# An emission order computed by a list scheduler, PSUM in single-bank tiles, and p loaded in 4 KB rows: attention feeding a swish MLP

## The chip, the cores and the metric

The kernel runs on one core of one Trainium2 chip. The metric is the device time of one execution in microseconds; I give the median of several runs with the lowest and highest. The kernel before took 307.49 us (306.49 to 308.46, 3 runs) when the prediction was made. In the profiles PE is TensorE, PEld its weight loads, DVE VectorE, ACT ScalarE, POOL GpSimd, and SP the engine that issues most transfers; a matmul's form such as 64*32 is the part of the array that it uses (rows*columns).

## The reference

Eight batches of eight heads, 576 positions of 64. A first attention packs keys and values into 32 rows per head with the queries p. A second one lets q attend to these rows, so its keys and its values are both the packed rows. The result, 4608 tokens of 512, goes through an MLP of width 2048 with `h * sigmoid(beta * h)`.

```
p_packed = sm_attn(p, k, v)               # 32 rows per head
out      = sm_attn(q, p_packed, p_packed)
x = out.transpose(0, 2, 1, 3).reshape(B * S, H * D)
h = x @ w_in                              # [4608,512] x [512,2048]
g = h * (1.0 / (1.0 + np.exp(-beta * h)))
return g @ w_out                          # [4608,2048] x [2048,512]
```

Both kernels use one idea: x is a product of the attention weights A2 and the packed rows, so the packed rows are multiplied by w_in first (W, small 64x32 tiles of the array), and h is A2 times W. beta is folded into W and divided out of w_out. In the profiles `w_ps` is that W product, `h_ps` the first and `o_ps` the second MLP product; `kT`, `qT`, `pT` are transposes; `s`, `z`, `pp` are scores, their sums and the packed rows.

## The kernel before

The order is written by hand: each phase interleaves one batch's MLP with the next batch's attention and the former batch's second product, by counts found by trial.

```python
self.ps_h = pool("ps_h", 2, space=PSUM)      # 2 tiles of 1 bank
self.ps_o = pool("ps_o", 2, space=PSUM)      # 2 tiles of 1 bank
self.ps_a = pool("ps_a", 2, space=PSUM)      # 2 tiles of 2 banks, all of the attention
...
def att(self, name, dtype=f32):
    n = 1024 if dtype == f32 else 2048       # two banks
...
def scores1(self, b):
    ps = self.att("s1_ps")
    for t in range(4):
        for c in range(NC): ...              # 16 matmuls into both banks
    nc.scalar.activation(E[:, 0:4, :], ps..., AF.Exp, scale=SCALE)   # then one activation
...
def fused_w(self, b, n):                     # W: eight 64*32 matmuls per group
    ps = self.att("w_ps").rearrange("p (r n) -> p r n", r=2)
    for c in range(NC):
        for r in range(2):
            self.mm(ps[32*c : 32*c+32, r, :], pp[64*r : 64*r+64, c, :],
                    self.w_in_bf[64*r : 64*r+64, c, cols], pos=(64*r, 32*c))
    ...                                      # one multiplication by beta on VectorE
...
nc.scalar.dma_start(self.p32[:], self.p.rearrange("b (g h) j d -> (h j) (b g) d", g=2))  # 256 B pieces
...
        attn("fused_w", nb, 0)               # the hand-made order, a few lines of one phase
        fill(6)                              # six steps of the former batch's second product
        main(10, 1)                          # one block of this batch's h, then one such step
        attn("weights2", nb)
```

The softmax here doesn't subtract the row's maximum and nothing guards it: scores larger than these inputs give would overflow.

Of the kernel before, what the change touches and what calls it, by code (L numbers as in the profile page):

```python
# [9 lines left out]
NP = 32  # L10
# [16 lines left out]
EXP_SET = "natural_log_exp_and_others"  # L27
SILU_SET = "silu_and_others"


class Kernel:
# [3 lines left out]
    def __init__(self, ctx, tc, q, k, v, p, w_in, w_out, beta, out):  # L35
# [16 lines left out]
        self.ps_a = pool("ps_a", 2, space=PSUM)  # L52
        self.x32, self.xbf = {}, {}
        self.st = {}
        self.g, self.grem = {}, {}
# [9 lines left out]
    def att(self, name, dtype=f32):  # L65
        n = 1024 if dtype == f32 else 2048
        return self.ps_a.tile([128, n], dtype, tag="att", name=name)


    def load(self, b, x, parts=1):  # L70
        nc, src = self.nc, self.src[x]
        t = self.in32.tile([128, 2304], f32, tag=f"{x}32", name=f"{x}32")
        n = 8 // parts
        for i in range(parts):
            h = slice(n * i, n * i + n)
            nc.sync.dma_start(
                t[:, 0:2048].rearrange("p (h e) -> p h e", h=8)[:, h],
                src[b, h, 0:SM, :].rearrange("h (p t) d -> p h (t d)", p=128),
            )
        for g in range(2):  # L80
            nc.sync.dma_start(
                t[64 * g : 64 * g + 64, 2048:2304].rearrange("p (h d) -> p h d", h=4),
                src[b, 4 * g : 4 * g + 4, SM:S, :].rearrange("h p d -> p h d"),
            )
        self.x32[b, x] = t

    def cast(self, b, x, *copies):

        t = self.x32.pop((b, x))
        o = self.inbf.tile([128, 2304], bf16, tag=f"{x}bf", name=f"{x}_bf")  # L90
        main = copies[:-1]
        n = 8 // len(main)
        for i, copy in enumerate(main):
            h = slice(n * i, n * i + n)
            copy(  # L95
                o[:, 0:2048].rearrange("p (t h d) -> p h t d", t=4, h=8)[:, h],
                t[:, 0:2048].rearrange("p (h t d) -> p h t d", h=8, t=4)[:, h],
            )
        copies[-1](o[:, 2048:2304], t[:, 2048:2304])
        self.xbf[b, x] = o  # L100


    def transpose_main(self, b, x, copies=None):
        ps = self.att(f"{x}T_ps", bf16)
        src = self.xbf[b, x]
        for c in range(NC):
            for t in range(4):
                o = 128 * (4 * c + t)
                i = 512 * t + 128 * c
                self.tp(ps[:, o : o + 128], src[:, i : i + 128], self.identr[:])  # L110
        xT = self.tr.tile([128, NC, S if x == "q" else SM], bf16, tag=f"{x}T", name=f"{x}T")
        copies = copies or [self.nc.vector.tensor_copy]
        n = NC // len(copies)
        for i, copy in enumerate(copies):
            c = slice(n * i, n * i + n)
            copy(xT[:, c, 0:SM], ps[:].rearrange("p (c n) -> p c n", c=NC)[:, c])  # L116
        self.st[b, x] = xT

    def transpose_rem(self, b):
        ps = self.att("remT_ps", bf16)  # L120
        for xi, x in enumerate("kq"):
            src = self.xbf[b, x]
            for u in range(2):
                o = 256 * xi + 128 * u
                i = 2048 + 128 * u
                self.tp(ps[:, o : o + 128], src[:, i : i + 128], self.identr[:])
        kTr = self.tr.tile([128, 2, 128], bf16, tag="kTr", name="kTr")
        self.nc.vector.tensor_copy(kTr[:], ps[:, 0:256].rearrange("p (u n) -> p u n", u=2))
        self.st[b, "kr"] = kTr
        self.nc.vector.tensor_copy(  # L130
            self.st[b, "q"][:, :, SM:S].rearrange("p (g u) n -> p u g n", u=2),
            ps[:, 256:512].rearrange("p (u g n) -> p u g n", u=2, g=2),
        )

    def exp_set(self):
        self.nc.scalar.preload_act_table_set(EXP_SET)  # L136

    def silu_set(self):
        self.nc.scalar.preload_act_table_set(SILU_SET)  # L139

    def scores1(self, b):
        nc = self.nc
        kT, kTr = self.st.pop((b, "k")), self.st.pop((b, "kr"))
        E = self.E1T[b % 2]
        pT = self.pT[:, 4 * b : 4 * b + 4, :]
        ps = self.att("s1_ps")
        for t in range(4):
            for c in range(NC):
                o = 256 * t + 64 * c
                self.mm(ps[:, o : o + 64], kT[:, c, 128 * t : 128 * t + 128], pT[:, c, :])  # L150
        nc.scalar.activation(  # L151
            E[:, 0:4, :], ps[:].rearrange("p (t e) -> p t e", t=4), AF.Exp, scale=SCALE
        )
        pr = self.att("s1r_ps")
        for u in range(2):
            self.mm(
                pr[:, 0:256].rearrange("p (g u e) -> p u g e", g=2, u=2)[:, u],
                kTr[:, u, :],
                pT.rearrange("p (g u) e -> p u g e", u=2)[:, u],
            )  # L160
        for g in range(2):
            nc.scalar.activation(
                E[64 * g : 64 * g + 64, 4, 128 * g : 128 * g + 128],
                pr[64 * g : 64 * g + 64, 128 * g : 128 * g + 128],
                AF.Exp,
                scale=SCALE,
            )

    def packed(self, b):

        nc = self.nc
        E = self.E1T[b % 2]
        v = self.xbf[b, "v"]
        ps = self.att("pp_ps")
        for r in range(2):
            for t in range(5):
                self.mm(
                    ps[64 * r : 64 * r + 64, 512:640].rearrange("p (c j) -> p c j", c=NC),
                    self.ones64[:],
                    E[:, t, :].rearrange("p (c r j) -> p r c j", c=NC, r=2)[:, r],  # L180
                    start=(t == 0),
                    stop=(t == 4),
                    pos=(0, 64 * r),
                )
        for c in range(NC):
            for t in range(5):
                i = 512 * t + 128 * c if t < 4 else 2048 + 128 * (c % 2)
                self.mm(
                    ps[:, 64 * c : 64 * c + 64],
                    v[:, i : i + 128],  # L190
                    E[:, t, 64 * c : 64 * c + 64],
                    start=(t == 0),
                    stop=(t == 4),
                )
        rz = self.sm.tile([128, 128], f32, tag="rz1", name="rz1")
        nc.vector.reciprocal(rz[:], ps[:, 512:640])  # L196
        pp = self.sm.tile([128, NC, NP], bf16, tag="pp", name="pp")
        for r in range(2):
            h = slice(64 * r, 64 * r + 64)
            nc.vector.tensor_tensor(  # L200
                pp[h],
                ps[h, 0:256].rearrange("p (c r j) -> p r c j", c=NC, r=2)[:, r],
                rz[h].rearrange("p (c j) -> p c j", c=NC),
                ALU.mult,
            )
        self.st[b, "pp"] = pp

    def scores2(self, b):
        nc = self.nc
        pp, qT = self.st[b, "pp"], self.st.pop((b, "q"))  # L210
        E = self.sm.tile([128, 2, S], bf16, tag="E2T", name="E2T")
        for lo, hi in ((0, SM), (SM, S)):
            ps = self.att("s2_ps").rearrange("p (r n) -> p r n", r=2)
            for c in range(NC):
                for r in range(2):
                    self.mm(
                        ps[32 * c : 32 * c + 32, r, 0 : hi - lo],
                        pp[64 * r : 64 * r + 64, c, :],
                        qT[64 * r : 64 * r + 64, c, lo:hi],
                        pos=(64 * r, 32 * c),  # L220
                    )
            nc.scalar.activation(E[:, :, lo:hi], ps[:, :, 0 : hi - lo], AF.Exp, scale=SCALE)  # L222
        self.st[b, "E2"] = E

    def norm2(self, b):
        nc = self.nc
        E = self.st[b, "E2"]
        rz = self.one.tile([128, 2, S], f32, tag="rz2", name="rz2")
        for lo, hi in ((0, SM), (SM, S)):
            ps = self.att("z2_ps").rearrange("p (r n) -> p r n", r=2)  # L230
            for r in range(2):
                self.mm(ps[:, r, 0 : hi - lo], self.bones[:], E[:, r, lo:hi])
            nc.scalar.activation(rz[:, :, lo:hi], ps[:, :, 0 : hi - lo], AF.Ln)  # L233
# [82 lines left out]
    def second(self, b):  # L316
# [3 lines left out]
        for group in groups:  # L320
            ps = {t: self.ps_o.tile([128, DM], f32, tag="o", name="o_ps") for t in group}
            for n in range(4):
                for t in group:
                    for ft in range(4 * n, 4 * n + 4):
                        self.second_mm(b, t, ft, ps[t])
                        if ft < FT - 1:
                            yield
# [350 lines left out]
```

## Time and profile before

| what | kernel before |
|---|---|
| time, median | 307.49 us |
| profiled span | 304.1 us |
| TensorE busy | 261.4 us, 86% |
| first MLP matmul of batch 0 | 36.39 us |
| last matmul ends | 299.47 us |
| ACT table loads | 26 |

"Busy" counts instructions with modelled ends, and a trace can lack some matmul records (this one has 2189 for 2225 weight loads); for one engine that has work the whole time the better measure is start to start. The lines themselves are in the prediction. Three more are used later. They are stretches of the kernel before (columns: stretch, length, busy us and instructions of PE, PEld, DVE, ACT, POOL, granted PE clock, DMA share, GB/s):

```profile
0.00:30.00 30.00, 18.13 (x157) 15.81 (x157) 11.40 (x26) 11.76 (x14) 10.48 (x16) 1.00 1.02 305
60.00:100.00 40.00, 36.02 (x280) 17.43 (x285) 21.36 (x29) 16.73 (x27) 13.30 (x11) 0.96 0.82 235
100.00:140.00 40.00, 33.60 (x314) 16.57 (x319) 19.91 (x22) 27.59 (x40) 7.30 (x8) 0.96 0.75 204
```

Between 60 and 140 us TensorE stands idle for about 10 us, although work of three batches is there. The clock column is no guide to the start: it shows 1.00 in the first 30 us, where sixteen transposes still took 1.67 us from start to start, against 0.89 later.

### The profile page before, as it was taken

How to read it: one execution, taken by the hardware profiler on the slowest of the kernel's cores; microseconds unless marked ns; L12 is line 12 of the kernel's file. 1: busy time of each engine (PE TensorE's matmuls, PEld its weight loads, DVE VectorE, ACT ScalarE, POOL GpSimd, SP SyncE). 2: the span in 40 equal slices, each digit the busy share in tenths (PEclk: the TensorE clock that was granted, in tenths of full speed). 3: DMA queues.
4: the chain of work that ended last, by engine and by line, in shares of the span. 5: the costliest groups of instructions: out<-in, count | busy, mean ns of one | idle time of the engine just before them, and what ended most of it. 6: DMA issues, size and time to landing. Idle time of an engine off the chain costs nothing.

```text
span 304.1 us, 5209 instructions
## 1 busy us (share of the span) xinstructions
PE 261.4 (86%) x2189; PEld 135.0 (44%) x2225; DVE 126.0 (41%) x168; ACT 165.4 (54%) x242; POOL 60.2 (20%) x58
## 2 busy tenths in 40 slices
PE   2768496587999889689999999999999999999993
PEld 2656134232456355236434643455346434444441
DVE  6332543558424573363345435443373346010121
ACT  1363587363521637886686667447865685435000
POOL 3136550015206206202600152005200000000000
PEclk9999999789999999989999999999999999999998
DMA  7999993199299594393011981069200010211112
GB/s 205 292 355 371 291 347 111 36 331 241 86 277 277 150 295 131 84 317 103 34 71 37 268 243 59 34 190 312 78 28 37 34 71 17 54 54 50 71 69 69
DMA packets 49655, 47.01 MB, mean 155 GB/s; under 512 B 16336, under 2 KB 40928, under 8 KB 49632
## 3 DMA queue, kind: packets, MB, share of 16 engines
q1 hardware_dynamic: 47536, 46.15, 51.5%
q10 hardware_dynamic: 2096, 0.53, 1.0%
q8 instruction: 17, 0.28, 0.4%
q14 instruction: 6, 0.05, 0.1%
HBM read 37.23 MB, written 9.44 MB: 153 GB/s over the span
## 4 chain that ended last, share of the span: by engine, by line
PE 76%; DVE 8%; ACT 8%; issue 4%; DMA 3%; ACTq 0%
PE o_ps L58 38%; PE h_ps L58 19%; PE w_ps L58 4%; PE pp_ps L58 3%; DMA p<-in_p_dram 3%; PE kT_ps L63 3%; DVE qT L116 3%; PE qT_ps L63 2%; ACT g_main L276 2%; ACT E2T L222 2%; DVE W_bf L259 2%; PE s_ps L58 2%; PE z_ps L58 1%; PE brow_ps L58 1%; DVE w_out_bf L436 1%
## 5 line engine op out<-in xcount | busy, mean ns | idle before, releaser
L58 PE MATMUL o_ps<-w_out_bf,g_main 128*128 128x512 bf16 x491 | 130.1, 383 | 4.0 <-DVE w_out_bf L436 2.4
L276 ACT ACTIVATE g_main<-h_ps 128x512 bf16<-128x512 f32 x128 | 75.0, 596 | 69.2 <-PE h_ps L58 62.6
L58 PE MATMUL h_ps<-A2T,W_bf 128*128 128x64 bf16 (+1 forms) x499 | 83.0, 289 | 6.5 <-DVE A2T L239 4.0
L58 PEld LDWEIGHTS <-g_main 128*128 128x128 bf16 x512 | 48.1, 98 | 57.5 <-issue 5.9
L307 DVE COPY o_sb<-o_ps 128x512 f32<-128x512 f32 x36 | 24.9, 691 | 86.3 <-PE o_ps L58 86.3
L58 PEld LDWEIGHTS <-W_bf 128*128 128x128 bf16 x512 | 31.9, 98 | 39.7 <-issue 18.3
L259 DVE TENSOR_TENSOR W_bf<-w_ps,beta_bc 128x1024 bf16<-128x1024 f32 x32 | 38.5, 1220 | 21.2 <-PE w_ps L58 20.5
L95 POOL CAST k_bf<-k 128x2048 bf16<-128x2048 f32 x7 | 13.3, 1893 | 120.3 <-DMA k<-in_k_dram 71.0
L58 PE MATMUL w_ps<-w_in_bf,pp 64*32 64x512 bf16 x256 | 14.3, 422 | 4.4 <-ACT rz L233 2.5
L196 DVE RECIPROCAL rz<-pp_ps 128x128 f32<-128x128 f32 x8 | 7.7, 957 | 24.8 <-PE pp_ps L58 24.8
L136 ACT ACT_TABLE_LOAD x13 | 16.7, 1283 | 2.0 <-issue 1.8
L116 DVE COPY kT<-kT_ps 128x2048 bf16<-128x2048 bf16 (+1 forms) x8 | 9.3, 1158 | 18.4 <-PE kT_ps L63 18.4
L139 ACT ACT_TABLE_LOAD x13 | 16.7, 1283 | 0.2
L95 POOL CAST v_bf<-v 128x2048 bf16<-128x2048 f32 x7 | 14.0, 1993 | 9.9 <-issue 3.9
L58 PEld LDWEIGHTS <-pp 64*32 64x32 bf16 x384 | 5.2, 90 | 23.1 <-issue 18.5
L58 PE MATMUL o_ps<-w_out_bf,g_rem 128*128 128x512 bf16 x64 | 15.3, 379 | 0.0
L116 DVE COPY qT<-qT_ps 128x2048 bf16<-128x2048 bf16 (+1 forms) x8 | 9.3, 1157 | 13.6 <-PE qT_ps L63 13.6
L95 POOL CAST q_bf<-q 128x2048 bf16<-128x2048 f32 x7 | 13.3, 1907 | 6.5 <-DMA q<-in_q_dram 6.5
L222 ACT ACTIVATE E2T<-s_ps 128x1024 bf16<-128x1024 f32 (+1 forms) x16 | 9.5, 649 | 7.6 <-PE s_ps L58 7.6
L151 ACT ACTIVATE E1T<-s_ps 128x1024 bf16<-128x1024 f32 x8 | 8.2, 1023 | 9.4 <-PE s_ps L58 9.3
L233 ACT ACTIVATE rz<-z_ps 128x1024 f32<-128x1024 f32 (+1 forms) x16 | 9.5, 648 | 6.7 <-PE z_ps L58 3.6
L294 ACT ACTIVATE g_rem<-h_ps 128x512 bf16<-128x512 f32 x16 | 9.3, 596 | 6.0 <-PE h_ps L58 5.6
(66 smaller groups left out, 199.3 us busy)
## 6 DMA issues: line engine op xcount, KB each, us to landing
out_dram<-o_sb SPq DMA_DIRECT2D x32, 256.0 KB, 2.3
k<-in_k_dram SPq DMA_DIRECT2D x7, 1024.0 KB, 7.7
q<-in_q_dram SPq DMA_DIRECT2D x7, 1024.0 KB, 9.9
v<-in_v_dram SPq DMA_DIRECT2D x7, 1024.0 KB, 8.6
w_in<-in_moe_w_in_dram SPq DMA_DIRECT2D x4, 1024.0 KB, 8.9
w_out<-in_moe_w_out_dram SPq DMA_DIRECT2D x4, 1024.0 KB, 7.9
k<-in_k_dram SPq DMA_DIRECT2D x2, 512.0 KB, 4.7
k<-in_k_dram SPq DMA_DIRECT2D x16, 64.0 KB, 7.4
```

The costliest lines, as they stand in the source:

```text
L58: return self.nc.tensor.matmul(out, lhsT, rhs, start=start, stop=stop, tile_position=pos, skip_group_check=True)
L63: return self.nc.tensor.matmul(out, in_, ident, is_transpose=True, skip_group_check=True)
L95: copy(o[:, 0:2048].rearrange("p (t h d) -> p h t d", t=4, h=8)[:, h], t[:, 0:2048].rearrange("p (h t d) -> p h t d", h=8, t=4)[:, h],)
L116: copy(xT[:, c, 0:SM], ps[:].rearrange("p (c n) -> p c n", c=NC)[:, c])
L136: self.nc.scalar.preload_act_table_set(EXP_SET)
L139: self.nc.scalar.preload_act_table_set(SILU_SET)
L222: nc.scalar.activation(E[:, :, lo:hi], ps[:, :, 0 : hi - lo], AF.Exp, scale=SCALE)
L233: nc.scalar.activation(rz[:, :, lo:hi], ps[:, :, 0 : hi - lo], AF.Ln)
L259: self.nc.vector.tensor_tensor(W[:, :, cols], ps, self.beta_bc[:, cols].unsqueeze(1).to_broadcast([128, 2, 512]), ALU.mult,)
L276: self.nc.scalar.activation(self.g[b][:, ft, :], ps[:], AF.Silu)
L294: self.nc.scalar.activation(self.grem[b // 2][:, 8 * half : 8 * half + 8, o : o + 64], ps[:].rearrange("p (f n) -> p f n", f=8), AF.Silu,)
L307: nc.vector.tensor_copy(o[:], ps[:])
```

## The change

The intent: let a program find the order. Each operation becomes a task with one engine, a guessed duration, its dependences, a rank and, where it needs a PSUM tile, a ring to take it from. A list scheduler walks through time and starts on each free engine the ready task of the lowest rank; the kernel is emitted in the order of these starts. The engines then run their streams in that order. PSUM is split into eight one-bank tiles (4 attention, 2 h, 2 o), so two-bank pieces become two pieces of one bank. The rest came with it: p in 4 KB rows at the head of k's queue (before, it had ScalarE's queue to itself and beta), filler matmuls where TensorE has nothing before 36 us, and exp and silu sorted by table set.

```diff
+TABLE_US = 1.3
+HOP_US = 0.2
+LAND_US = 2.0
+WARM_UNTIL = 36.0
+class Planner:
+    def run(self):
  ... (cut: for every engine that is free at "now")
+                can = [t for t in ready[e] if t.ready <= now + 1e-9 and room(t)]
  ... (cut: choice of the ACT table set)
+                if not can:
+                    if e == "PE" and now < WARM_UNTIL:
+                        self.filler()
+                        free[e] = now + 0.11
+                        moved = True
+                    continue
+                start(min(can, key=lambda t: t.rank))
  ...
-        self.ps_a = pool("ps_a", 2, space=PSUM)
+        self.ps_a = pool("ps_a", 4, space=PSUM)
  ...
-        n = 1024 if dtype == f32 else 2048
+        n = 512 if dtype == f32 else 1024
  ... (cut: every operation as a task; the one of W, now eight pieces of four matmuls)
+        def fused_w(m):
+            n, r = m // 2, m % 2
+            st[b, "w", m] = ps = self.att("w_ps")
+            for c in range(NC):
+                self.mm(ps[32*c : 32*c+32, :], st[b, "pp"][64*r : 64*r+64, c, :],
+                        self.w_in_bf[64*r : 64*r+64, c, 512*n : 512*n+512], pos=(64*r, 32*c))
+        for m in range(8):
+            w = self.task(("w", b, m), "PE", 0.27, lambda m=m: fused_w(m), [...], rank + 7, takes="att")
+            self.task(("W", b, m), "DVE", 0.68, lambda m=m: scaled_w(m), [...], rank + 7, ends=[w])
  ...
-        nc.scalar.dma_start(self.p32[:], self.p.rearrange("b (g h) j d -> (h j) (b g) d", g=2))
+            nc.sync.dma_start(self.p32[:], self.p.rearrange("b h (a s) d -> (b h a) s d", s=16))
```

## The prediction

> **What bounds the kernel now.** I read the page first (busy shares, the forty slices, the chain that ended last), then the busy time of every engine in four stretches of the span, then the timeline of the first 60 us, and last the TensorE timeline of one later batch.
>
> ```profile
> PE 261.4 (86%) x2189; PEld 135.0 (44%) x2225; DVE 126.0 (41%) x168; ACT 165.4 (54%) x242; POOL 60.2 (20%) x58
> PE   2768496587999889689999999999999999999993
> PE 76%; DVE 8%; ACT 8%; issue 4%; DMA 3%; ACTq 0%
> ```
>
> TensorE sets the end, but the slices show that the kernel is two kernels: up to about the 18th slice (137 us) PE has holes, after it hardly any. The stretches put numbers on that (columns: stretch, its length, busy us and instructions of PE, PEld, DVE, ACT, POOL, then granted PE clock, DMA share, GB/s):
>
> ```profile
> 0.00:36.39 36.39, 20.13 (x168) 16.49 (x170) 15.61 (x29) 15.46 (x18) 14.26 (x18) 1.00 1.04 301
> 36.39:138.07 101.68, 85.29 (x763) 41.62 (x775) 50.26 (x64) 57.45 (x89) 25.83 (x23) 0.95 0.73 210
> 138.07:299.47 161.40, 155.96 (x1262) 76.90 (x1281) 59.41 (x74) 92.45 (x136) 20.08 (x18) 1.00 0.29 89
> ```
>
> 36.39 us is the first MLP matmul of batch 0, 138.07 us the first transpose of batch 4, 299.47 us the last matmul. Busy PE is not PE at its peak, so I count the work instead, by spacings from dense places of the timeline: 128x512 matmuls start 0.2157 us apart (16 in 3.45 us), transposes 0.0557 us (16 in 0.89), the 64-column MLP remainder 0.031 us, a group of eight 64*32 matmuls for W takes 0.44 us between two other kinds. Per program: o 576 x 0.2157 = 124.2; h 256 x 0.2157 = 55.2; 288 transposes 16.0; remainder 7.9; W 32 x 0.44 = 14.1; packed sums and products 10.4; the other scores and sums 12.0. Together 240 us. By the instruction order, 84 of these lie before 138.07 us and 156 behind it. So from 138.07 on the kernel does 156 us of work in 161.4 us (97%), and before it loses 138 - 84 = 54 us. Only those 54 us can be won by an order.
>
> Where they go is in the timeline:
>
> ```profile
> 9.56 1.49 DVE L370 CAST p_dup<-p 128x1024 bf16<-128x1024 f32 x2 [2.71 <-DMA p<-in_p_dram]
> 24.14 3.78 PE L58 MATMUL brow_ps<-b_safe,ident 16*128 16x128 f32 x16
> 36.39 3.34 PE L58 MATMUL h_ps<-A2T,W_bf 128*128 128x512 bf16 x8 [3.11 <-DVE A2T L239]
> 65.82 0.38 PE L58 MATMUL o_ps<-w_out_bf,g_main 128*128 128x512 bf16 x1 [1.21 <-DVE w_out_bf L436]
> ```
>
> p arrives at 9.56 us; sixteen beta matmuls needed only later stand in front of batch 0's second scores; the first eight MLP matmuls take 0.42 us each, twice the later spacing, a cold TensorE; and at 66 us PE waits for w_out, whose scaling was emitted behind batch 1's attention.
>
> **What the Trainium skill says.** "TensorE: Matmul & The Clock Gate", Part 1: the array runs at half clock until some 3.4 us of sustained activity. The trace agrees: 16 transposes take 1.89 us at 11 us and 0.89 us at 110 us, and h spacing falls from 0.42 to 0.22 us near 40 us. The clock column shows 1.00 for the first stretch, so I trust the durations, not that column. "DMA: Bandwidth & Descriptors", "Why small descriptors are slow": a fixed cost per packet. p is loaded in 256 B pieces and takes 8.33 us for 512 KB, beside k; a 256 KB store in 2 KB rows lands in 2.3 us. "ScalarE: Activation LUTs", "What ACT_TABLE_LOAD costs": 1283 ns and a drain of about the same. The trace has 26 loads of 1283 ns, but the next activation starts within 0.1 us, so I count 1.3 us. "TensorEngine Tiling (Array Packing)", Key Properties: changing the tiling mode drains TensorE. In the trace o gives way to W with about 0.10 us lost; I use that.
>
> **The change part by part.**
> The operations stay nearly the same (same matmul counts per kind), the order is new, and I read it from the instruction order of the changed kernel.
>
> 1. p in 4 KB rows, issued first on the same queue as k. Estimate from rates of this trace: issue at about 1.2 us, 2.3 us fixed as the store, plus 512 KB at about 350 GB/s, 1.5 us: lands near 5 us rather than 9.6. DMA engines were full in the first 36 us (share 1.04), so the 1.0% of queue q10 (about 3 us of all 16 engines) shrinks to 1.3, and what follows arrives some 1.5 us sooner: v near 16 us, w_in block 0 near 18.7 instead of 20.2.
>
> 2. 165 filler matmuls (128x128), about 130 of them before the first MLP matmul. Warm they cost 0.056 us each, 9 us in all, placed where the list found no task. They halve the PE pieces of the first 36 us that lie in the chain: transposes 1.89 + 1.72 + 1.05, scores 1.05, packed 2.36, W 1.61 + 0.68 = 10.4 us, so 5 us less.
>
> 3. beta spread in four pieces of 4, moved between waits: the 3.72 us at 24 us leave the chain. v is cast in halves on DVE (0.68 each), not half on ACT (PE then waited for v until 22.96 us).
>
> By hand: v cast by 17.5 us, packed 18.5, normalised 19.3, second scores 20, then ACT: two exps, two logs, two exps of 0.6 plus remainders and hops, A2 complete at about 25.5; W block 0 is ready by 23. With 1.5 us for orders that fit less well, the first MLP matmul comes at **27 us** instead of 36.4. Work done by then: 6 us.
>
> 4. Batch 0's MLP runs as 16 + 2 activations of 0.61 us: ACT-bound for 11.5 us, to **38.5 us**, with batch 1's transposes in its holes.
>
> 5. w_out is scaled as it lands, o of batch 0 fills batch 1's attention. The queue order is k, q, v of batch 1, then w_out: after w_in at about 28 us, three loads of nearly 4 us and four of 3 us end at about 52 us. From 38.5 to **50 us** PE has batch 1's attention (3 us), some W (2 us) and o of the blocks landed (8 us) for 11.5 us, with waits. By 50 us about 28 of the 240 us are done; the kernel before has 17 done by then.
>
> 6. Finer pieces cost PE: 55 stretches of 64*32 matmuls instead of 37, at two changes of 0.10 us each, 18 x 0.2 = 3.6, say 4 us. ACT has 16 table loads instead of 26, 12.8 us less, but loses some fixed cost to halves (two of about 0.61 us for one of 1.02); DVE likewise (two of about 0.65 for one of 1.22). Neither lies on the path later: per batch ACT needs about 22 us of 30.
>
> Sum: 50 + (240 + 4 - 28) / 0.97 = 50 + 223 = 273 us for the last matmul; copy and store behind it as before 4.6; span 277 to 278; the timed runs lie 3.4 us above the profiled span (307.49 against 304.1): **281 us**, about 9% less.
>
> **The rivals.**
> (a) The gain is that of the start only, and later stretches come out even. For it: the kernel before is 97% dense after 138 us. Against it: its order from 36 to 138 us loses 28 us (102 us for about 74 of work), with waits like the one at 66 us and a clock of 0.50 from 56.5 to 63.3 us. If the middle stretch stays lossy because w_out comes late: 290 to 295 us.
> (b) A static order made from fixed durations misfires: transfers come later than its 2.9 us per megabyte and 2.0 us landing assume, and an in-order engine waits at the head while other work is ready. For it: in the trace k, q and v take 7.7 to 9.9 us from issue to landing, and queued loads need near 4 us each rather than 3.65. Against it: after 55 us loads lead by a batch. 2 to 6 us: 283 to 287.
> (c) The fillers don't warm the array (128 columns, half the time idle once warm): the start keeps its 5 us, 286 us.
> (d) ACT or DVE becomes the bound through smaller pieces, or mode changes cost more than 0.1 us. DVE before is 41%, and splits add perhaps 10 us. Unlikely; 5 us.
> (e) Everything fits and PE runs at 99% from 45 us on: 272 us.
>
> **Range and chances.** 281 us, 272 to 293 in 8 of 10. Against slower speaks that no engine gets more than 5% more work; a 2% gain (301 us) needs only the start's 9 us less part of it. Faster 0.95, same 0.04, slower 0.01.
>
> **What would show it.** p_dup starting near 5 us; transposes near 0.9 us per 16 before 15 us; first h near 27 us; 16 table loads; w_out scaled between 43 and 54 us; no clock of 0.5 after 40 us; from 55 us on PE busy 97%; 64*32 groups of four costing below 0.3 us. Wrong would be: first h after 32 us, a stretch under 90% busy after 60 us with PE waiting for DMA or DVE, or an o spacing clearly above 0.2157 us.

## The result, and the profile after

The changed kernel took **286.75 us** (285.96 to 288.39, 4 runs), the kernel before in the same rounds 306.99 us (305.13 to 308.46, 4 runs). The ratio is 0.9351, with an interval of 0.9281 to 0.942. A second set of runs on another chip gave 286.84 us and 0.9368. The prediction was 281 us with a range of 272 to 293. Direction and range held; the middle was 6 us too low. (Every run takes 1.8 us more than its own profiled span; the 3.4 us of the prediction compare a median with the span of another, faster run.)

The page of the kernel after, its first lines, its slices of the span for PE, and its chain of waits:

```profile
span 284.2 us, 5670 instructions
PE 269.2 (95%) x2382; PEld 138.8 (49%) x2382; DVE 127.4 (45%) x232; ACT 151.5 (53%) x280; POOL 59.9 (21%) x58
PE   7957999999999999999999999999999999989993
PE 76%; DMA 13%; DVE 5%; SPq 3%; POOL 1%; issue 1%; POOLq 0%; DVEq 0%
```

The holes are gone from the fifth slice (about 30 us) on, but for a small one near the end, where before they lasted to the eighteenth. ACT has left the chain, and DMA has entered it. The longest pieces of the chain's first 50 us (start, length) show that the start is now set by what arrives, the blocks of w_out last:

```profile
2.12 6.30 DMA k<-in_k_dram
...
11.35 9.05 DMA w_in<-in_moe_w_in_dram
...
25.93 10.12 DMA q<-in_q_dram
...
37.44 11.50 DMA w_out<-in_moe_w_out_dram
```
The same stretches as before, for the kernel after:

```profile
0.00:30.00 30.00, 23.08 (x317) 19.40 (x318) 17.48 (x37) 13.76 (x24) 12.05 (x16) 1.00 0.98 311
60.00:100.00 40.00, 40.00 (x344) 19.73 (x345) 20.18 (x35) 22.44 (x42) 10.31 (x10) 1.00 0.85 242
100.00:140.00 40.00, 40.00 (x342) 19.57 (x340) 14.98 (x26) 22.99 (x44) 6.66 (x6) 1.00 0.44 129
140.00:220.00 80.00, 79.87 (x700) 38.74 (x699) 35.16 (x64) 44.33 (x86) 19.97 (x18) 1.00 0.42 131
```

From 60 to 140 us TensorE is never without an instruction, and from 140 us to the end it waits for under 2 us in all. The middle that lost time before is full, so rival (a) of the prediction is out. The transposes of batch 4 start at 111.10 us instead of 137.91, almost 27 us earlier; from there to the last matmul it is 168.4 us instead of 161.4, partly because one batch of packed rows and of W more lies behind them in the new order. So the whole gain is made before that point. A full engine may be full of slower work. The page's rows of the W product say so, before and after (columns: line, engine, operation, tiles, count, busy us, mean ns, idle before it):

```profile
L58 PE MATMUL w_ps<-w_in_bf,pp 64*32 64x512 bf16 x256 | 14.3, 422 | 4.4 <-ACT rz L233 2.5
```

```profile
L164 PE MATMUL w_ps<-w_in_bf,pp 64*32 64x512 bf16 x256 | 21.5, 393 | 3.1 <-POOL w_in_bf L786 1.6
```

The same 256 matmuls hold TensorE 7.2 us longer, though the mean of one is shorter: more of the time is not overlapped. The timeline of the kernel after shows how (start, length):

```profile
118.11 0.40 PE L164 MATMUL w_ps<-w_in_bf,pp 64*32 64x512 bf16 x4
118.44 0.60 PE L164 MATMUL o_ps<-w_out_bf,g_main 128*128 128x512 bf16 x2
118.97 0.40 PE L164 MATMUL w_ps<-w_in_bf,pp 64*32 64x512 bf16 x4
119.30 1.04 PE L164 MATMUL o_ps<-w_out_bf,g_main 128*128 128x512 bf16 x4
...
121.56 0.41 PE L164 MATMUL w_ps<-w_in_bf,pp 64*32 64x512 bf16 x8
121.91 0.82 PE L164 MATMUL o_ps<-w_out_bf,g_main 128*128 128x512 bf16 x3
```

From the start of four W matmuls to the start of the next work pass 0.33 us; eight of them, two pieces that happened to be neighbours, take 0.35 us. Four cost what eight cost. In the trace the four start within 0.010 us (118.107 to 118.117) and the eight within 0.024, so they run side by side; a piece of four, by its `pos`, uses the row half r of the array alone, and two pieces together use both. And the two o matmuls between two pieces take 0.53 us from start to start, where two of them need 0.43 (two spacings of 0.2157): 0.10 us go at the change.

The start of the kernel after, the lines of the timeline that answer to those of before:

```profile
4.89 1.29 DVE L713 CAST p_dup<-p 128x1024 bf16<-128x1024 f32 x2 [0.89 <-DMA p<-in_p_dram]
7.13 1.06 PE L169 MATMUL pT_ps<-identr,p_dup 128*128 128x128 bf16 x16
17.15 0.69 DVE L239 CAST v_bf<-v 128x1024 bf16<-128x1024 f32 x1 [2.08 <-DMA v<-in_v_dram]
17.76 0.28 DVE L311 COPY kTr<-remT_ps 128x256 bf16<-128x256 bf16 x1
18.10 0.29 PE L164 MATMUL s1r_ps<-pT,kTr 128*128 128x128 bf16 x2 [2.70 <-DVE kTr L311]
28.53 0.40 PE L164 MATMUL w_ps<-w_in_bf,pp 64*32 64x512 bf16 x4 [1.61 <-POOL w_in_bf L786]
29.46 1.21 PE L164 MATMUL h_ps<-A2T,W_bf 128*128 128x512 bf16 x4
```

p is there at 4.89 us, as predicted. Then comes what a fixed order does: VectorE waits 2.08 us at the head of its stream for the second half of v, with the small copy of kTr behind it, and TensorE waits 2.70 us for that copy. The list had v arriving earlier than it does. (What this wait costs is another question: in e4 and e11 below it is gone, and the MLP starts no sooner.) At 28.53 us TensorE waits once more, for a cast of w_in. The first MLP matmul starts at 29.46 us.

### The profile page after: what moved, and what is told of

It reads as the page before. It is cut to its first block, busy times and chain, and to the rows that moved or that the text cites. A ratio compares the mean times of both kernels' runs of the same rounds, so it can differ in the third digit from the quotient of the medians.

```text
span 284.2 us, 5670 instructions
## 1 busy us (share of the span) xinstructions
PE 269.2 (95%) x2382; PEld 138.8 (49%) x2382; DVE 127.4 (45%) x232; ACT 151.5 (53%) x280; POOL 59.9 (21%) x58
## 4 chain that ended last, share of the span: by engine, by line
PE 76%; DMA 13%; DVE 5%; SPq 3%; POOL 1%; issue 1%; POOLq 0%; DVEq 0%
PE o_ps L164 42%; PE h_ps L164 17%; PE w_ps L164 5%; DMA w_out<-in_moe_w_out_dram 4%; DMA q<-in_q_dram 4%; DMA w_in<-in_moe_w_in_dram 3%; PE hr_ps L164 2%; DMA k<-in_k_dram 2%; PE z_ps L164 2%; PE s_ps L164 2%; PE qT_ps L169 2%; PE kT_ps L169 2%; DVE o_sb L636 2%; SPq L219 2%; DVE A2T L488 1%; PE pp_ps L164 1%
## 5 line engine op out<-in xcount | busy, mean ns | idle before, releaser
L164 PE MATMUL h_ps<-A2T,W_bf 128*128 128x512 bf16 x256 | 69.1, 382 | 0.4 <-ACT g_main L578 0.4
L550 DVE TENSOR_TENSOR W_bf<-w_ps,beta_bc 128x512 bf16<-128x512 f32 x64 | 40.6, 684 | 19.6 <-PE w_ps L164 19.6
L450 ACT ACTIVATE E2T<-s_ps 128x512 bf16<-128x512 f32 x16 | 8.7, 595 | 35.9 <-PE s2r_ps L164 29.2
L179 ACT ACT_TABLE_LOAD x16 | 20.5, 1283 | 1.0 <-PEq L858 0.7
L164 PE MATMUL warm_ps<-identr 128*128 128x128 bf16 x165 | 15.0, 244 | 1.9 <-DVE bones L681 1.9
L279 DVE COPY kT<-kT_ps 128x1024 bf16<-128x1024 bf16 x15 | 9.8, 685 | 11.5 <-PE kT_ps L169 11.5
L488 DVE TENSOR_TENSOR A2T<-E2T,rz 128x512 bf16<-128x512 bf16 (+1 forms) x24 | 14.7, 648 | 0.2 <-ACT rz L483 0.2
L164 PEld LDWEIGHTS <-identr 128*128 128x128 bf16 x165 | 12.2, 111 | 4.9 <-DVE bones L681 1.9
L483 ACT ACTIVATE rz<-rz 128x512 f32<-128x512 f32 (+1 forms) x24 | 12.6, 523 | 0.8
L598 ACT ACTIVATE g_rem<-hr_ps 128x512 bf16<-128x512 f32 x16 | 8.9, 595 | 4.8 <-PE hr_ps L164 4.8
L169 PEld LDWEIGHTS <-k_bf 128*128 128x128 bf16 x144 | 9.4, 98 | 3.9 <-issue 0.3
```

The source lines that it names most:

```text
L164: return self.nc.tensor.matmul(out, lhsT, rhs, start=start, stop=stop, tile_position=pos, skip_group_check=True)
L169: return self.nc.tensor.matmul(out, in_, ident, is_transpose=True, skip_group_check=True)
L179: self.nc.scalar.preload_act_table_set(SETS[mode])
L279: self.copy[engine](st[b, x, "T"][:, 2 * i : 2 * i + 2, 0:SM], st[b, x, "ps", i][:].rearrange("p (c n) -> p c n", c=2),)
L450: nc.scalar.activation(st[b, "E2"][:, i, 0:SM], st[b, "s2", i][:], AF.Exp, scale=SCALE)
L483: nc.scalar.activation(rz, rz, AF.Exp, scale=-1.0)
```

## The experiments

The theory after the result: the gain is made of the start (about 7 us) and of a middle that is dense because the list never lets TensorE run out; and some 6 us of it are given back by W in pieces of four and by transfer times that the list has wrong. The rivals: the one-bank tiles would bring the density in any order; the fillers and the 4 KB rows do little; and differences of a few us are chance of the order.

| run | time, median (range), us | ratio to the kernel before |
|---|---|---|
| a0_again: the kernel after | 286.84 (286.65–287.73) | 0.9368 |
| e1_no_fillers | 284.13 (282.88–285.58) | 0.9271 |
| e2_p_256 | 287.83 (287.44–288.06) | 0.9392 |
| e3_w_merged | 288.97 (288.15–289.95) | 0.9432 |
| e4_dma_times | 286.09 (285.92–286.78) | 0.9326 |
| e5_before_p4k | 306.63 (303.55–307.18) | 0.9955 |
| e6_before_p4k_fill | 300.84 (300.30–303.60) | 0.9828 |
| e7_before_split | 297.61 (294.76–298.30) | 0.9685 |
| e8_merged_times | 289.43 (286.62–290.29) | 0.9414 |
| e9_w_pairs | 280.33 (279.63–281.19) | 0.9141 |
| e10_order_no_fill | 286.37 (285.05–286.53) | 0.9327 |
| e11_hop | 282.03 (281.27–282.11) | 0.9190 |

Each has five runs; all results were correct. a0 to e3 shared a chip (before: 306.06 us), so did e4, e5, e6 and e8 (306.88 us), and e7 and e9 to e11 (307.42 us). The half-widths of the intervals are about 0.45 to 0.7% of the time, 1.3 to 2.2 us.

**a0_again**, the kernel after without an edit, as the partner of the first group.

> The changed kernel unchanged, as the yardstick for the other three of this chip. Every theory: 0.935 of the kernel before, 286 to 288 us, first MLP matmul of batch 0 near 29.5 us.

286.84 us: the result repeats. The profiled run shows how far one and the same program can shift at the start. One cast on VectorE, in the kernel after and then in a0:

```profile
1.33 0.55 DVE L677 CAST identr<-ident 128x128 bf16<-128x128 f32 x1 [1.33 <-POOL ident masks.py:199]
```

```profile
1.33 2.29 DVE L677 CAST identr<-ident 128x128 bf16<-128x128 f32 x1 [1.33 <-POOL ident masks.py:199]
```

In a0 the first h comes at 30.28 us and the transposes of batch 4 at 112.46 us, 0.8 and 1.4 us later than in the kernel after. Why the cast is long in one run is not shown. All later runs of the new kernel have the long one, so their starts are to be compared with a0.

**e1_no_fillers**: the list plans no fillers.

```diff
-WARM_UNTIL = 36.0
+WARM_UNTIL = 0.0
```

> All 165 filler matmuls taken out, same order otherwise. Theory 'the fillers keep the array warm, and the start is partly bound by TensorE': transposes at 0.107 us each before 15 us, first MLP matmul 2 to 3 us later and its first eight matmuls at 0.42 us spacing, end 3 to 4 us later (about 290 us). Rival 'the start is bound by transfers, so a cold array hides behind them': the end moves by less than 1 us. Rival 'the fillers are in the way': 1 us earlier.

The start became slower, as expected: first MLP matmul at 31.17 us (a0: 30.28), and the array was cold until about 36.5 us (eight h matmuls took 3.19 us). Yet the kernel ended 2.7 us sooner. My expectation assumed the same order otherwise, and that was false: the fillers take time in the plan, so without them the list orders other work otherwise, W among it. So the run does not say what fillers are worth. e10 below does it cleanly.

**e2_p_256**: p in 256 B pieces again, on the same queue, the rest of the new kernel unchanged (the placing of pT follows).

```diff
-nc.sync.dma_start(self.p32[:], self.p.rearrange("b h (a s) d -> (b h a) s d", s=16))
+nc.sync.dma_start(self.p32[:], self.p.rearrange("b (g h) j d -> (h j) (b g) d", g=2))
```

> p loaded in 256 B pieces again (same queue, still first), the rest as in the changed kernel. Theory 'the small pieces take some 1.7 us more of the 16 DMA engines, and the start is a chain of transfers': every later load and the end shift by 1.5 to 2 us (288.5 us), p lands at 6.5 us or later instead of 4.9. Rival 'hidden': first k cast a little later, end unchanged within 0.5 us.

1.0 us slower, first h at 30.97 us (a0: 30.28). The direction held and the size was smaller than expected; a difference of 1.0 us is inside the intervals of the two runs, so it is not settled. One sign failed outright: p_dup starts at 5.29 us (a0: 5.05), not at 6.5 or later. From issue to landing p takes 4.1 us in 256 B pieces and 3.7 us in 4 KB rows on this queue, against 8.3 us in the kernel before, in the same 256 B pieces on ScalarE's queue beside k. So p comes early through its place in the queue, and hardly through the rows.

**e3_w_merged**: the W product again in four groups of eight, each taking two banks at once in the list.

```diff
-        for m in range(8):
-            w = self.task(("w", b, m), "PE", 0.27, lambda m=m: fused_w(m), ..., takes="att")
-            self.task(("W", b, m), "DVE", 0.68, ..., ends=[w])
+        for n in range(4):
+            w = self.task(("w", b, n), "PE", 0.35, lambda n=n: fused_w(n), ..., takes="att")   # two slots
+            for r in range(2):
+                self.task(("W", b, 2 * n + r), "DVE", 0.68, ..., ends=[(w, r)])
```

> The W product as tasks of eight matmuls into two banks at once, r alternating as in the kernel before, the rest of the changed kernel as it is. Theory 'a piece of four 64*32 matmuls holds TensorE as long as one of eight (0.33 against 0.34 us), and each change of mode adds 0.1 us': 1.2 to 1.4 us less per batch, 8 to 10 us less in all, 277 to 279 us. Rival 'taking two banks at once makes the matmuls wait for VectorE and the order loses what the pieces win': 284 to 288 us, with TensorE idle in front of W.

2.1 us slower than a0, so the rival held for this edit. The waits of TensorE in this run (line waited for, total us, times, longest) against the same two in the kernel after:

```profile
PE h_ps L166 <- ACT g_main L583: 4.6, 8, 0.7
...
PE w_ps L166 <- DVE W_bf L553: 3.2, 7, 1.7
```

```profile
PE h_ps L164 <- ACT g_main L578: 0.4, 2, 0.3
...
PE w_ps L164 <- DVE W_bf L550: 0.2, 1, 0.2
```

Asking for two free banks at once moved the whole order, and TensorE waited 7.2 us longer on these two. What cheaper W groups are worth can't be read from a run in which everything else moved. That led to e9.

**e4_dma_times**: the transfer times in the list set to what the trace shows, nothing else.

```diff
-    lb 0.1; k,q,v halves 1.5; whole 2.9; remainder 0.75; w_in, w_out blocks 3.0
+    lb 1.2; k,q,v halves 1.75; whole 3.1; remainder 0.95; w_in, w_out blocks 2.75
```

> The changed kernel with the list's own transfer times set to what its trace shows (first issue 1.2 us in, 1.75 us for 512 KB, 0.95 for the tails, 2.75 for 1 MB of weights, 3.1 for 1 MB of k, q, v), so that the emitted order fits real landings. Theory 'the start is a chain of transfers, and the order only has to follow': the 2.7 us wait of TensorE at 15 us goes, first MLP matmul up to 1 us earlier, end 0 to 1.5 us earlier (285.5 to 287). Rival 'the misfit of the planned landings costs the start': 3 to 5 us earlier (282 to 284).

286.09 us, −0.75 against a0. The theory (0 to −1.5) held, but the difference is within the noise. The wait of 2.70 us for kTr is gone, as expected, and yet the scores behind it start at 18.23 us (18.10 in the kernel after, 17.98 in a0). One MLP matmul came at 27.27 us, the next only at 28.89, behind a wait for W.

**e8_merged_times**: e3 and e4 together.

> W in tasks of eight and the measured transfer times together. Both theories: the sum of the two single effects, 275 to 279 us, fastest of all. Rival: no better than the merged W alone.

289.43 us: not the sum of the two effects, and no better than e3, as the rival had it.

**e5_before_p4k** and **e6_before_p4k_fill**: the old kernel with p in 4 KB rows and on k's queue, so two changes at once, without and with fillers put at fixed places of the start (128 of them by hand).

```diff
-        nc.scalar.dma_start(self.p32[:], self.p.rearrange("b (g h) j d -> (h j) (b g) d", g=2))
+        nc.sync.dma_start(self.p32[:], self.p.rearrange("b h (a s) d -> (b h a) s d", s=16))
  ... (e6 only)
+        self.keep_warm(30)          # after the constants; 8 to 30 more after each step of batch 0
```

> The kernel before with only p in 4 KB rows, still first, on the queue of k. Theory 'its start waits for p until 9.6 us': p_dup starts near 5 us, first MLP matmul 2 to 4 us earlier (33 to 34 us), end about 3 us earlier (0.99). Rival 'the next wait takes its place' (k, the cold array, the beta matmuls): under 1 us.

> As the previous one, with 128 fillers placed by hand between the first steps. Theory 'a cold array costs the old start 5 us': first MLP matmul at 29 to 31 us, its matmuls at 0.22 us spacing, end 7 to 9 us earlier than the kernel before (0.975). So the start alone would give under half of the 20 us, and the order between 36 and 138 us the rest. Rival 'most of the gain is the start': 15 us or more earlier (0.95).

e5: 306.63 against 306.88 us, ratio 0.9955 with an interval of 0.9883 to 1.0027; the first h moved from 36.39 to 35.04 us. p_dup started at 6.77 us, not near 5, and its transposes at 9.54 us, behind the beta matmuls that hold TensorE from 5.85 us: in the hand-made order the next wait takes the place of the one for p. e6: ratio 0.9828 with an interval of 0.9766 to 0.9891, 6 us by the medians. Its first h came at 35.56 us, not at the 29 to 31 expected, but the array was warm by then (four h in 1.02 us against eight in 3.34). Only 2.3 us of its gain lie in its trace (transposes of batch 4 at 135.60 us against 137.91, span 301.8 against 304.1): the profiled run, 303.6 us, was the slowest of its five, and the profiled run of the kernel before, 305.9 us, a fast one. So e6 is a gain of 3 to 7 us by its interval, not settled further.

**e7_before_split**: the old order with one-bank tiles alone.

```diff
-        self.ps_a = pool("ps_a", 2, space=PSUM)
+        self.ps_a = pool("ps_a", 4, space=PSUM)
-        n = 1024 if dtype == f32 else 2048
+        n = 512 if dtype == f32 else 1024
  ... scores1, for example:
-        ps = self.att("s1_ps")
-        for t in range(4): ...
-        nc.scalar.activation(E[:, 0:4, :], ps..., AF.Exp, scale=SCALE)
+        for i in range(2):
+            ps = self.att("s1_ps")
+            for t in range(2): ...
+            nc.scalar.activation(E[:, 2 * i : 2 * i + 2, :], ps..., AF.Exp, scale=SCALE)
  ... (likewise transposes, pp and its sums, s2, z2, pT, brow; W keeps its groups of eight, over two tiles)
```

> The kernel before, its own order, with the attention's PSUM tiles split into four of one bank and every operation on them in halves: the split alone. Theory 'the split costs fixed time on ACT and VectorE and gives nothing without a new order': 0 to 4 us slower than the kernel before (1.00 to 1.013). Rival 'finer buffers let the engines overlap by themselves': 4 us or more faster (under 0.985).

297.61 us, −9.8 us, ratio 0.9685. My theory (0 to +4 us) fell and the rival held: the finer buffers, with the operations on them in halves, overlap by themselves, in an order that was tuned for the coarse ones. (Which of the two does it, the tiles or the halves, the run can't say.) Some waits of TensorE (us, times, longest), kernel before and then e7:

```profile
PE z_ps L58 <- ACT E2T L222: 4.3, 5, 1.9
...
PE s_ps L58 <- DVE qT L116: 3.3, 6, 1.1
PE w_ps L58 <- ACT rz L233: 2.5, 3, 1.1
...
PE pp_ps L58 <- ACT E1T L151: 1.9, 2, 1.0
```

```profile
PE z_ps L58 <- ACT E2T L225: 2.2, 5, 1.5
...
PE w_ps L58 <- ACT rz L236: 1.0, 3, 0.4
```

These waits, for data that come out of a tile or for the tile itself, are halved or gone from the view's longest: the first half can be read while the second is written, and a consumer starts on half the data. Others took part of their place (z_ps behind E1T 1.2 us, h_ps behind g_main 3.0 instead of 1.9). The idle time of TensorE in the whole trace falls from 38.1 to 28.8 us. First h comes 3.8 us sooner (32.56 us), the transposes of batch 4 5.6 us sooner (132.26 against 137.91), and after that about 0.7 us per batch is gained (batch 4 to batch 7: 90.0 against 92.1 us). The Trainium skill points this way, in "Perfetto Trace Analysis", section "Optimizing Tensor Performance": independent groups should go round different PSUM banks, so that emptying one overlaps filling the next. That a two-bank tile should be split follows from it only in part, as the kernel before went round two such tiles. I had not drawn on it in the prediction.

**e9_w_pairs**: the order of the changed kernel kept as the list made it, but of each two pieces of W the first is not emitted at its own place; both are emitted together at the place of the second. No time in the list changes.

```diff
         def fused_w(m):
-            n, r = m // 2, m % 2
-            st[b, "w", m] = ps = self.att("w_ps")
+            if m % 2 == 0:
+                return
+            n = m // 2
+            for r in range(2):
+                st[b, "w", 2 * n + r] = self.att("w_ps")
             for c in range(NC):
-                self.mm(ps[32*c : 32*c+32, :], ...)
+                for r in range(2):
+                    self.mm(st[b, "w", 2 * n + r][32*c : 32*c+32, :], ...)
  ... (the multiplication by beta likewise)
```

> The changed kernel in its own order, but each pair of W pieces (four matmuls each) emitted together at the place of the second, r alternating; the two VectorE products likewise. Unlike the merged tasks of an earlier run, nothing else moves. Theory 'a piece of four costs what eight cost': TensorE time of W in the later batches falls from 2.5 to about 1.5 us a batch, end 5 to 8 us earlier (279 to 282 us). Rival 'what W wins, waits for VectorE take back, as the merged tasks showed': within 2 us of the changed kernel, with W matmuls waiting for VectorE.

**280.33 us, the best of all, 6.4 us below the kernel after** (6.0 below e10 on the same chip). The theory of the W pieces is confirmed, and its rival, that holding two banks would bring new waits, fell: W waits 1.0 us for VectorE in all, and the gain stands. The kernel after has 37 stretches of four W matmuls, e9 none. The timeline at the same place:

```profile
117.17 0.41 PE L164 MATMUL w_ps<-w_in_bf,pp 64*32 64x512 bf16 x8
117.51 1.90 PE L164 MATMUL o_ps<-w_out_bf,g_main 128*128 128x512 bf16 x8
119.34 0.41 PE L164 MATMUL w_ps<-w_in_bf,pp 64*32 64x512 bf16 x8
119.69 1.04 PE L164 MATMUL o_ps<-w_out_bf,g_main 128*128 128x512 bf16 x4
```

Eight matmuls hold TensorE for 0.34 us, half as much per matmul. The busy time of the W matmuls alone in the same stretch, 128 of them in each (columns: stretch, length, busy us and count, clock, DMA share, GB/s), in the kernel after and then in e9:

```profile
140.00:279.00 139.00, 10.91 (x128) 1.00 0.30 93
```

```profile
140.00:279.00 139.00, 7.63 (x128) 0.99 0.31 95
```

3.3 us for four batches, 0.82 per batch (2.7 to 1.9 us, where 2.5 to 1.5 was expected). That the whole batch got shorter by more is seen in the transposes of k, batch 4 and batch 7, kernel after and then e9:

```profile
111.10 1.06 PE L169 MATMUL kT_ps<-identr,k_bf 128*128 128x128 bf16 x16
...
209.14 1.06 PE L169 MATMUL kT_ps<-identr,k_bf 128*128 128x128 bf16 x16
```

```profile
109.73 0.94 PE L169 MATMUL kT_ps<-identr,k_bf 128*128 128x128 bf16 x14
...
204.28 0.89 PE L169 MATMUL kT_ps<-identr,k_bf 128*128 128x128 bf16 x13
```

98.0 us against 94.6 us for three batches, 1.16 us per batch; the difference to 0.82 fits the three fewer stretches of 64*32 matmuls per batch (15 against 24 in these three batches) at 0.10 us each. The page gives e9 the smaller busy share, 92% against 95%, but its trace lacks 38 matmul records (hence x14 and x13 above), so the two shares can't be compared.

**e10_order_no_fill**: the fillers stay in the plan, so the order is the same, but nothing is emitted for them.

```diff
     def keep_warm(self):
-        if self.warm is None:
-            self.warm = self.ps_o.tile([128, DM], f32, tag="o", name="warm_ps")
-        self.mm(self.warm[:, 0:128], self.identr[:], self.identr[:])
+        return
```

> The changed kernel's order kept exactly, fillers planned but not emitted (the earlier run without fillers also got another order in the later batches). Theory 'fillers help the start by about 1 us and the earlier gain of 2.7 us came from the order': 287 to 289 us, first MLP matmul 1 to 2 us later. Rival 'the fillers hold up real work': 283 to 285 us.

286.37 us against 286.84 and 286.75 with them: ratio 0.9327 against 0.9368 and 0.9351, intervals that overlap. Neither expectation was quite met: fillers neither help nor hurt at the end by an amount that the runs resolve. Yet they do warm the array. The transposes of p in e10, beside those of the kernel after shown above:

```profile
7.30 1.91 PE L169 MATMUL pT_ps<-identr,p_dup 128*128 128x128 bf16 x16
9.00 1.61 PE L164 MATMUL brow_ps<-b_safe,ident 128*128 128x128 f32 x8
```

Sixteen take 1.70 us from start to start, against 0.89. The stretch of the first 30 us:

```profile
0.00:30.00 30.00, 17.99 (x178) 13.44 (x180) 18.49 (x37) 13.80 (x24) 11.96 (x16) 0.78 0.98 315
```

The clock column shows 0.78 instead of 1.00 (and 1.00 for the cold start of the kernel before, so the durations are the evidence), and eight h matmuls at 31.45 us take 3.17 us. Still the first h comes at 29.47 us, against 29.46 in the kernel after and 30.28 in a0: both have the same transfers ahead of it, and DMA is busy 98% of the time in both. What TensorE does cold it seems to do in waits that it has anyway. By batch 4 e10 is even ahead (110.53 us; 111.10 in the kernel after, 112.46 in a0), and from there to batch 7 it needs the same 98.0 us.

**e11_hop**: only the delay that the list assumes between engines.

```diff
-HOP_US = 0.2
+HOP_US = 0.25
```

> The changed kernel with the list's assumed delay between engines 0.25 us instead of 0.2: no operation changes, only the order. Theory 'orders of this list differ by a few us by chance': 283 to 290 us, with the later batches' W pieces falling otherwise. Rival 'the order is robust': within 0.5 us of 286.8.

282.03 us, 4.3 us below e10 on the same chip, from an edit that changes no operation of the work, only the order (and 169 fillers instead of 165). The theory that orders differ by a few us by chance held. Here the 2.70 us wait for kTr at the start is gone, but the start gains nothing by it: first h at 29.42 us, transposes of batch 4 at 112.29 us. W happens to fall less often into pieces of four (28 stretches of four instead of 37): its busy time between 140 and 279 us is 9.24 us, between the 10.91 of the kernel after and the 7.63 of e9. That explains 1.7 us of the gain in the later part; the rest of it is not settled.

## Why the prediction was right or wrong

**Right in kind.** TensorE sets the end, the work on it is nearly constant, and only the lost time before 138 us can be won. This held: of the prediction's signs, p at 5 us (4.89), sixteen transposes in 0.89 us before 15 us (7.13 to 8.02; the 1.89 that the prediction set beside 0.89 is a length, from start to start it was 1.67), 16 table loads, w_out scaled between 43 and 54 us (from 43.57 on) and a dense TensorE after 55 us are there. There are 12.8 us fewer of table loads on ACT; what they gave the end has no run of its own.

**The sum, term by term.** 273 us for the last matmul were predicted and 279.5 measured:

- *First h at 27 us: measured 29.46.* The hand estimate allowed 1.5 us for an ill-fitting order. What it got wrong is when things are ready: w_in block 0 came at 20.46 us (20.21 before, not the 18.7 forecast), A2's first two parts were complete at 26.72 and not at 25.5, and W block 0 at 27.45 and not at 23. The list then put two pieces of W for a later block in front of h, and one waited 1.61 us for its cast. This is rival (b), in part. The wait of 2.70 us for v is not shown to cost anything: without it (e4, e11) h came at 27.27 and 28.89, and at 29.42 us. The array was cold once, from about 30.3 to 33.6 us.
- *28 us of work done by 50 us: it was about 23.* Counted as in the prediction: the matmuls before 50 us in the trace (32 h, 17 o, 89 transposes, one batch of W, two of packed rows) by the prediction's durations. Batch 0's MLP ended at 44.7 us instead of 38.5, as it started later and had the next batch's transposes between. That is some +5 us.
- *Finer pieces, 18 stretches x 0.2 us, 4 us in all: about 10.* **This is the step that was mis-sized.** I counted the changes of mode and took for granted that four W matmuls cost half of eight, "below 0.3 us". They cost 0.33 against 0.34 us. From start to start, W after 64.7 us takes 15.2 us for 192 matmuls, 0.079 each; in the dense part of the kernel before it is 0.043. For the 224 of batches 1 to 7 this is 8 us, and the changes another 2. That is +6 us, and e9 gave 6.0 to 6.4 us back by undoing just this.
- *97% density after 50 us, 7 us lost: nearly none.* From 60 us on TensorE waits for under 2 us in all. That is some −5 us, and I had it in rival (e) only.
- *3.4 us from span to time: 2.6*, of which 1.8 are in every run and the rest is the spread of the runs.

273 + 5 + 6 − 5 is 279, where 279.5 was measured, and 286.75 follows with the tail of 4.7 us and the 2.6 us. So two errors were partly cancelled by a third, which is luck; the range covered it. The −5 us is what was left over when the other terms were counted.

**Wrong about where the gain comes from.** The prediction put the order first and the tiles among the costs. e7 shows that the tiles alone, in the old order, bring 9.8 of the 20 us. It also gave 1.5 us to the 4 KB rows and 5 us to a warm start. In the new kernel the rows are worth about 1 us, inside the noise (e2), and the fillers nothing that the runs resolve (e10): the transfers are what the start waits for. And p's early landing, which the prediction put down to the cost of small pieces, came from the queue: in 256 B pieces on k's queue it lands within 0.4 us of the rows (e2). In the old kernel rows, queue and fillers together bring 3 to 7 us (e6). Rival (c), that the fillers would fail to warm the array, was wrong in its reason: they warm it.

**Left open.** What the computed order alone is worth has no run of its own: no kernel ran the list with two-bank tiles. By difference it is what remains of 20 us after 9.8 for the tiles (8 to 11 by the interval) and about 1 for p, some 9 us, with the W pieces already taken off; effects need not add. How good the best order could be is open as well: e11 shows that the list's result moves by 4 to 5 us with an assumed delay, and e9 with the delay of e11 was not run.

## What to carry to other kernels

Before computing an order, try to split two-bank PSUM tiles into single banks: here it brought about half of the gain by itself, and it needs no scheduler. A scheduler that cuts work finer must know what a short group costs: four 64*32 matmuls took as long as eight, and putting pairs back together was worth 6 us with the rest of the order kept. And a list's order carries some us of chance, so an edit that lets it replan tests the new order along with the edit; keep the order fixed where an effect of a few us is to be shown.

## What the Trainium skill lacked or had wrong

- "TensorEngine Tiling (Array Packing)", Key Properties, names the drain at a change of mode but gives no cost: here about 0.10 us at a change from 128*128 to 64*32.
- "ScalarE: Activation LUTs", What ACT_TABLE_LOAD costs: the load takes 1283 ns here too, but the drain of about 1380 ns beside it is not seen. In the kernel before a load runs from 142.67 us for 1.28 us and the next activation starts at 143.97.
- "TensorE: Matmul & The Clock Gate", Part 1: the half clock is seen as stated (eight h in 3.17 us, cold). What it does not say is that a cold start can hide behind transfers: fillers brought sixteen transposes from 1.70 to 0.89 us and left the time at 286.8 against 286.4 us.
- "Perfetto Trace Analysis", Optimizing Tensor Performance: going round the banks is advised without a size. Here splitting two-bank tiles alone gave 9.8 us of 307.4 (ratio 0.9685).
- I found no page on how to choose a fixed order for engines that each run their own stream in order, or on what a wait at a bad place in it costs: a copy that was ready stood behind a cast that waited 2.08 us for v, and TensorE stood idle for 2.70 us, without a gain at the first h where the wait was gone (e4, e11).
